# Cached attention for one new token: the softmax of a step in two halves, and the last V in two loads

## The chip, the cores and the metric

The kernel runs on one core of one Trainium2 chip. A core has a matrix engine (TensorE, PE in the profile, with its weight loads listed as PEld), a vector engine (VectorE, DVE), a scalar engine (ScalarE, ACT), GpSimd (POOL) and SyncE (SP), which here only issues transfers. Sixteen transfer engines move data between device memory and the core. SBUF is the core's working memory, PSUM the memory in which matmuls leave their results. [...]

The metric is the device time of a whole execution in microseconds (us). The profile is of one execution.

## The reference

```python
xn = _layernorm(x)                         # x: 2 x 1 x 512
q  = (xn @ wq)                             # 2 batches x 32 heads x 128
scores = einsum("bhqd,bhkd->bhqk", q, k_cache) * (Dh ** -0.5)   # 8192 rows a head
p  = softmax(scores, axis=-1)
o  = einsum("bhqk,bhkd->bhqd", p, v_cache)
out = x + o.reshape(B, Sq, H * Dh) @ wo + relu(xn @ w1) @ w2
```

There is one query per batch and head, against 8192 rows of K and V of 128 numbers each, in bfloat16. K and V are 134 MB each, and each number is used once. The weights `wq`, `wo`, `w1` and `w2` are 12 MB together.

## The kernel before

The 64 pairs of batch and head are taken four at a time (`U = 4`), so there are 16 steps (`NP`). In a step the 128 partitions hold the four heads, 32 partitions each, and every partition holds 256 of its head's rows (`KB = 256`, index `kk`). One load of 8.4 MB brings a step's K into the buffer `ks`, another its V into `vs`. There is one buffer for each, not two.

**SP's queue** (lines 161 to 188) issues all the loads, in this order: K of step t, V of step t, K of step t+1 and so on. Before K of step t it waits for the last transposes of step t-1 (semaphore `pT[7]`, line 167). Before V of step t it waits for the last V matmul of step t-1 (`sW`, line 177). The last K is loaded in two halves. After the last transposes the weights `w1`, `w2` and `wo` go into the room of `ks` (lines 179 to 184).

**A step on PE** (lines 286 to 319). First 256 transposes of K (line 265), in 32 groups of eight, each group into one of four PSUM tiles `tp`. VectorE and ScalarE copy the groups to SBUF as `kT` (line 394, ScalarE the groups in `ON_ACT`). From group 28 on, scores of early groups are woven in (`LAG`). Then the remaining scores (line 272): 256 small matmuls that write into `Sc`, two banks of PSUM, 128 values of `kk` in each, four heads beside each other. For the softmax, VectorE takes each head's maximum over the first 128 `kk` after group 15 of the scores (`EARLY`, `sS0`) and over the other 128 after group 31 (`sS`), into the two columns of `mcol` (line 441). PE transposes both columns (line 303), VectorE reduces them to one negated maximum per head, `mx` (line 446), PE spreads it over the partitions (line 306), ScalarE copies it to `nm` (line 488) and makes four exps over 256 columns each (line 492), which also give the sum of each partition in `RS`. When all four are done (`sP`), PE runs the 256 V matmuls (line 311) into one accumulator `ot`. After the last one SP may issue the next V, and ScalarE copies the result to `OTf` (line 502).

GpSimd copies each step's four queries to `q4` (line 227) after the scores of the step before are done. It then also raises `dKb`, the second K semaphore, for those steps whose K comes in one load (line 229).

**The end** (lines 321 to 387). PE adds up the denominators over partitions (line 324), VectorE takes the reciprocal and multiplies (lines 453 and 456), while PE works on the first dense layer (line 338). Then come a transpose, a selection, and the projections by `w2` and `wo` (line 365), which are added into the same PSUM columns, and the store.

The order is written out by hand: there is no planner, and each engine's program is one loop over steps with semaphore waits. The loops of PE, VectorE and ScalarE keep the values to wait for in registers (`counters`, `advance`).

Of the kernel before, what the change touches and what calls it, by code (L numbers as in the profile page):

```python
# [11 lines left out]
U = 4  # L12
EG = 8
NG = 32
REP = 16
LAG = 28
EARLY = 16
ON_ACT = (0, 3, 5)


# [1 line left out]
def kernel(  # L22
# [79 lines left out]

    prm = sb([P, KB, U], bf16, "prm")
    mcol = sb([P, 2], bf16, "mcol")
    mx = sb([1, U], bf16, "mx")
    nm = sb([P, U], f32, "nm")
    RS = sb([P, NP], f32, "RS")
    OTf = sb([P, N], f32, "OTf")
    RD = sb([P, N], f32, "RD")
    OTn = sb([P, Bsz, H], bf16, "OTn")  # L110
    Ob = sb([H, Bsz, Dh], bf16, "Ob")
    OX = sb([P, WJ, Bsz], bf16, "OX")
# [8 lines left out]

    S = Sc[:].rearrange("p (k u) -> p k u", u=U)
    trp = ms[0:1, 0:P].bitcast(bf16)
    bc = ms[:, 480:480 + U]


    dX, dO, dQ, dW1, dW2 = sem("dX"), sem("dO"), sem("dQ"), sem("dW1"), sem("dW2")
    dKa, dKb, dV = sem("dKa"), sem("dKb"), sem("dV")
    sG, sI, sQ, sQ1 = sem("sG"), sem("sI"), sem("sQ"), sem("sQ1")
    sV, sA, sE = sem("sV"), sem("sA"), sem("sE")  # L130
    sS0, sS, sT, sB, sW = sem("sS0"), sem("sS"), sem("sT"), sem("sB"), sem("sW")
    pT = [sem(f"pT{e}") for e in range(HG)]
    kR = [sem(f"kR{e}") for e in range(HG)]
    sM, sX, sP, sO, sN = sem("sM"), sem("sX"), sem("sP"), sem("sO"), sem("sN")
# [26 lines left out]

    @(lambda f: f(nc.sync))
    def _(sp):
        for t in range(NP):
            rows = slice(t * P, (t + 1) * P)
            if t > 0:
                sp.wait_ge(pT[HG - 1], NH * t)
            if t < NP - 1:
                sp.dma_start(ks[:], K_all[rows, :]).then_inc(dKa, 16)
            else:  # L170
                for i, d in enumerate((dKa, dKb)):
                    half = slice(i * SLOT // 2, (i + 1) * SLOT // 2)
                    sp.dma_start(ks[:, half], K_all[rows, half]).then_inc(d, 16)
            if t == 0:
                sp.wait_ge(sQ, 2)
            else:
                sp.wait_ge(sW, t)
            sp.dma_start(vs[:], V_all[rows, :]).then_inc(dV, 16)
        sp.wait_ge(pT[HG - 1], NH * NP)
        sp.dma_start(w1_sb, B_w1.rearrange("(p kt) f -> p kt f", kt=KT)).then_inc(dW1, 16)  # L180
        sp.dma_start(w2_sb, B_w2.rearrange("(p j) n -> p j n", j=FJ)).then_inc(dW2, 16)
        for c in range(NC):
            sl = slice(cuts[c], cuts[c + 1])
            sp.dma_start(wo_sb[:, sl, :], wo_v[:, sl, :]).then_inc(piece[c][0], 16)
        sp.wait_ge(sE, 1)
        sp.dma_start(
            out.rearrange("b s (c p) -> (b s c) p", p=P), osb[:]
        ).then_inc(dO, 16)


    def counters(eng, kind):
        regs = [nc.alloc_register(kind, f"count{i}_{kind.name}") for i in range(1 + NH)]
        eng.reg_mov(regs[0], 0)
        for i in range(NH):
            eng.reg_mov(regs[1 + i], i + 1)
        return regs[0], regs[1:]

    def advance(eng, h):
        for r in h:
            eng.reg_add(r, r, NH)  # L200

    @(lambda f: f(nc.gpsimd))
    def _(g):
# [19 lines left out]
        g.wait_ge(sV, 100)  # L223
        for t in range(NP):
            if t > 0:
                g.wait_ge(sS, t)
            g.tensor_copy(q4[:], qb[:, U * t:U * t + U]).then_inc(sQ1, 1)  # L227
            if t < NP - 1:
                g.wait_ge(dKa, 16 * (t + 1)).then_inc(dKb, 16)
        g.wait_ge(dO, 16).then_inc(sG, 1)  # L230


# [1 line left out]
    def _(pe):  # L234
# [33 lines left out]
        def scores(e):  # L268
            for i in range(EG):
                kk = e * EG + i  # L270
                n = min(REP, BK - kk % BK)
                t = pe.matmul(  # L272
                    Sc[:, U * kk:U * (kk + n)],
                    lhsT=kT[e][:, i, :],
                    rhs=rep(q4[:], n),
                    start=True,
                    stop=True,
                )
            if e == EARLY - 1:
                t.then_inc(sS0, 1)  # L280
            if e == NG - 1:
                t.then_inc(sS, 1)

        reg, h = counters(pe, mybir.EngineType.PE)
        with pe.Fori(16, NL + 1, 16) as n16:
            pe.reg_add(reg, reg, 1)
            pe.wait_ge(dKa, n16)
            pe.wait_ge(sQ1, reg)
            for e in range(NG):
                if e == NG // 2:  # L290
                    pe.wait_ge(dKb, n16)
                if e >= 4:
                    pe.wait_ge(kR[(e - 4) % HG], h[(e - 4) // HG])
                transposes(e)
                if e >= LAG:
                    scores(e - LAG)
            for e in range(NG - LAG, NG):
                if e >= NG - 4:
                    pe.wait_ge(kR[e % HG], h[e // HG])
                scores(e)  # L300
            pe.wait_ge(sM, reg)
            for i in range(2):
                t = pe.transpose(trp[:, i * P:(i + 1) * P], mcol[:, i:i + 1], identb[:])  # L303
            t.then_inc(sT, 1)
            pe.wait_ge(sX, reg)
            pe.matmul(bc, lhsT=onesb[:], rhs=mx[:], start=True, stop=True).then_inc(sB, 1)  # L306
            pe.wait_ge(sP, reg)
            pe.wait_ge(sO, reg)
            pe.wait_ge(dV, n16)
            for kk in range(KB):  # L310
                t = pe.matmul(  # L311
                    ot[:, 0:U * REP],
                    lhsT=vs[:, kk * Dh:(kk + 1) * Dh],
                    rhs=rep(prm[:, kk, :], REP),
                    start=(kk == 0),
                    stop=(kk == KB - 1),
                )
            t.then_inc(sW, 1)
            advance(pe, h)

        pe.wait_ge(sI, 2 + U)
        dbp = Sc[:, 0:N].rearrange("p (t u) -> p t u", u=U)
        for u in range(U):
            t = pe.matmul(dbp[:, :, u], lhsT=onesh[:, u, :], rhs=RS[:], start=True, stop=True)  # L324
        t.then_inc(sH, 1)
        for k in range(KT):
            pe.matmul(
# [16 lines left out]
                )  # L344
        i.then_inc(sF, 1)

        pe.wait_ge(sV, 102)
        tO = tp[0][0:H, 0:Bsz, :]
        for b in range(Bsz):
            t = pe.transpose(tO[:, b, :], OTn[:, b, :], identb[:])  # L350
        t.then_inc(sH, 1)
        pe.wait_ge(sV, 103)
        for dq in range(DQ):
            t = pe.matmul(
                ox.rearrange("p (b j) -> p b j", b=Bsz),
# [19 lines left out]
        pe.wait_ge(dW2, 16)  # L375
        for j in range(FJ):
            project(w2_sb, j, hT)
        pe.wait_ge(sV, 104)
        for c in range(NC):
            pe.wait_ge(*piece[c])  # L380
            for j in range(cuts[c], cuts[c + 1]):
                t = project(wo_sb, j, OX, j == WJ - 1)
        t.then_inc(sH, 1)
        pe.wait_ge(sV, 105)
        pe.transpose(
            tp[1][0:Bsz * KT, 0, :], yT[:].rearrange("p b c -> p (b c)"), identb[:]
        ).then_inc(sH, 1)
# [10 lines left out]
    def _(v):  # L398
# [31 lines left out]
            tpq.rearrange("p l (g b) -> p l g b", b=Bsz),  # L430
        ).then_inc(sV, 93)

        reg, h = counters(v, mybir.EngineType.DVE)
        with v.Fori(0, NP):
            v.reg_add(reg, reg, 1)
            kcopies(v, False, h)
            for i, (lo, hi, s) in enumerate(((0, EARLY * EG, sS0), (EARLY * EG, KB, sS))):
                v.wait_ge(s, reg)
                for u in range(U):
                    own = slice(u * HP, (u + 1) * HP)  # L440
                    m = v.tensor_reduce(  # L441
                        out=mcol[own, i:i + 1], in_=S[own, lo:hi, u], axis=AX.X, op=ALU.max
                    )
            m.then_inc(sM, 1)
            v.wait_ge(sT, reg)
            v.tensor_reduce(  # L446
                out=mx[:], in_=trp.rearrange("o (i u m) -> o u i m", i=2, u=U),
                axis=AX.XY, op=ALU.max, negate=True,
            ).then_inc(sX, 1)
            advance(v, h)  # L450

        v.wait_ge(sH, 1)
        v.reciprocal(out=RD[:], in_=Sc[:, 0:N]).then_inc(sV, 1)
        v.wait_ge(sV, 101)
        v.wait_ge(sO, NP + 1)
        v.tensor_tensor(
            out=OTn[:].rearrange("p b h -> p (b h)"), in0=OTf[:], in1=RD[:], op=ALU.mult
        ).then_inc(sV, 1)
        v.wait_ge(sF, 1)
        v.tensor_scalar(  # L460
# [15 lines left out]
    def _(a):  # L476
# [2 lines left out]
            out=rstd[:], in_=mv[:, 1:2], func=ACTF.Sqrt, bias=eps_t[:Bsz], scale=1.0  # L479
        ).then_inc(sA, 1)  # L480

        a.copy(nm[:, 0:1], eps_t[:]).then_inc(sO, 1)
        reg, h = counters(a, mybir.EngineType.Activation)
        with a.Fori(0, NP) as t:
            a.reg_add(reg, reg, 1)
            kcopies(a, True, h)
            a.wait_ge(sB, reg)
            a.copy(nm[:], bc).then_inc(sN, 1)  # L488
            a.wait_ge(sN, reg)
            for u in range(U):  # L490
                own = slice(u * HP, (u + 1) * HP)
                x = a.activation(  # L492
                    out=prm[own, :, u],
                    in_=S[own, :, u],
                    func=ACTF.Exp,
                    bias=nm[own, u:u + 1],
                    scale=1.0,
                    accum_out=RS[own, bass.ds(t, 1)],
                )
            x.then_inc(sP, 1)  # L500
            a.wait_ge(sW, reg)
            a.copy(OTf[:, bass.ds(t * U, U)], ot[:, 0:U]).then_inc(sO, 1)  # L502
            advance(a, h)
# [1 line left out]
_INS = ['A_x', 'A_k_cache', 'A_v_cache', 'A_wq', 'A_wo', 'B_x', 'B_w1', 'B_w2']  # L505
_OUTS = [((2, 1, 512), 'bfloat16')]
# [25 lines left out]
```

## Time and profile before

| | |
|---|---|
| median of 8 runs | 696.02 us (692.76 to 698.48) |
| profiled execution | 698.76 us |
| its span, first to last instruction | 696.7 us |
| mean granted clock of PE | 0.893 |
| busy: PE, DVE, ACT | 548.3, 259.7, 269.9 us |
| read from device memory | 280.50 MB, 403 GB/s over the span |
| K transposes (line 265) | 4096, 247.4 us busy |
| scores (line 272) | 4096, 136.4 us busy |
| V matmuls (line 311) | 4096, 155.2 us busy; PE idle before them 59.3 us |
| exps (line 492) | 64, 817 ns each, of which 248 ns is the reading of the accumulator |
| maxima over 128 columns (line 441) | 128, 290 ns each |
| from issue to landing, K and V | median 24.8 and 22.2 us |

Busy time is the sum over instructions of one engine. [...] A line of a group ends with the idle time of the engine just before that group and with what ended it. In the row of slices, the span is cut in 40 equal parts and each digit is a share in tenths. `SPq` is SP's queue of transfers, and a wait there is a load that could not be issued yet. The chain is followed back from the last instruction, at each step to what released it.

### The profile page before, as it was taken

The numbers are of one execution on the slowest core, as the hardware profiler recorded it, in microseconds if no ns is written. First come the engines' busy times: TensorE is split into PE (matmuls) and PEld (weight loads), VectorE is DVE, ScalarE is ACT, GpSimd is POOL, SyncE is SP. The second block draws the span as 40 slices with busy tenths as digits, with TensorE's granted clock in tenths as the row PEclk, the third lists the DMA queues.
The fourth block names the chain that finished last, engine by engine and source line by source line (L and its number), as shares of the span: only waits on it lengthen the run. The fifth ranks groups of instructions, "written<-read, shape, count | busy, mean of one in ns | idle before, by whom it ended". The sixth has DMA issues, their size and how long they took to land.

```text
span 696.7 us, 26564 instructions
## 1 busy us (share of the span) xinstructions
PE 548.3 (79%) x12635; PEld 533.4 (77%) x12635; DVE 259.7 (37%) x481; ACT 269.9 (39%) x371; POOL 7.1 (1%) x30
## 2 busy tenths in 40 slices
PE   2494986967699696868879686977969696796968
PEld 0294986967688696868879686977969696796967
DVE  1071360715326071623517062441707153160711
ACT  1061433616333361624335262433527153251710
POOL 2000000000000000000000000000000000000000
PEclk9786998989989898989989898998989898898987
DMA  9999599999989999999999999899999999999992
GB/s 399 444 416 412 201 421 421 421 440 440 380 365 421 421 421 421 421 425 418 421 410 433 421 421 421 361 421 421 444 399 421 421 421 421 403 391 410 421 397 117
DMA packets 5789, 280.64 MB, mean 403 GB/s; under 512 B 658, under 2 KB 660, under 8 KB 916
## 3 DMA queue, kind: packets, MB, share of 16 engines
q1 hardware_dynamic: 5776, 280.50, 94.8%
q8 instruction: 8, 0.13, 0.1%
q10 hardware_dynamic: 4, 0.00, 0.0%
q14 instruction: 1, 0.01, 0.0%
HBM read 280.50 MB, written 0.00 MB: 403 GB/s over the span
## 4 chain that ended last, share of the span: by engine, by line
DMA 47%; PE 47%; ACT 3%; issue 1%; DVE 1%; ACTq 0%; SPq 0%
DMA ks<-in_A_k_cache_dram 47%; PE tp L265 34%; PE Sc L272 6%; PE ot L311 6%; ACT prm L492 2%; PE Sc L365 1%; DVE mcol L441 1%; ACT L394 1%; PE ms L338 0%; ACT kT L394 0%; DVE mx L446 0%; PE ms L303 0%; PE Sc L324 0%; PE ms L306 0%; ACT nm L488 0%
## 5 line engine op out<-in xcount | busy, mean ns | idle before, releaser
L394 DVE COPY kT<-tp 128x1024 bf16<-128x1024 bf16 x320 | 211.0, 688 | 295.0 <-PE tp L265 289.4
L265 PE MATMUL tp<-identb,ks 128*128 128x128 bf16 x4096 | 247.4, 222 | 38.7 <-DMA ks<-in_A_k_cache_dram 35.8
L265 PEld LDWEIGHTS tp<-identb,ks 128*128 128x128 bf16 x4096 | 237.2, 100 | 40.8 <-DMA ks<-in_A_k_cache_dram 37.3
L394 ACT COPY kT<-tp 128x1024 bf16<-128x1024 bf16 x192 | 190.1, 1013 | 86.7 <-PE tp L265 84.6
L311 PE MATMUL ot<-prm,vs 128*128 128x64 bf16 x4096 | 155.2, 207 | 59.3 <-ACT prm L492 59.3
L311 PEld LDWEIGHTS ot<-prm,vs 128*128 128x128 bf16 x4096 | 153.3, 108 | 60.6 <-ACT prm L492 60.6
L272 PE MATMUL Sc<-q,kT 128*128 128x64 bf16 (+8 forms) x4096 | 136.4, 191 | 4.6 <-issue 4.6
L272 PEld LDWEIGHTS Sc<-q,kT 128*128 128x128 bf16 x4096 | 132.4, 98 | 4.7 <-issue 4.7
L441 DVE TENSOR_REDUCE mcol<-Sc 32x1 bf16<-32x128 f32 x128 | 37.1, 290 | 89.8 <-PE Sc L272 88.5
L488 ACT COPY nm<-ms 128x4 f32<-128x4 f32 x16 | 2.6, 163 | 160.8 <-PE ms L306 160.8
L502 ACT COPY OTf<-ot 128x4 f32 x16 | 2.6, 162 | 158.0 <-PE ot L311 158.0
L492 ACT ACTIVATE prm<-Sc,nm 32x256 bf16<-32x256 f32 x64 | 52.3, 818 | 2.7
L394 ACT ACT_TABLE_LOAD x16 | 20.5, 1283 | 2.8 <-issue 2.7
L303 PE MATMUL ms<-identb,mcol 128*1 128x128 bf16 x32 | 4.5, 222 | 20.7 <-DVE mcol L441 20.7
L303 PEld LDWEIGHTS ms<-identb,mcol 128*1 128x1 bf16 x32 | 1.4, 81 | 22.1 <-DVE mcol L441 22.1
L492 ACT ACTIVATION_READ_ACCUMULATOR prm<-Sc,nm x64 | 15.8, 248 | 0.0
L244 PE MATMUL ot<-vs,xz 128*16 128x512 bf16 x32 | 9.4, 466 | 8.1 <-DMA vs<-in_A_wq_dram 8.1
L244 PEld LDWEIGHTS ot<-vs,xz 128*16 128x16 bf16 x32 | 3.3, 105 | 13.8 <-issue 11.4
L306 PEld LDWEIGHTS ms<-mx,onesb 1*128 1x128 bf16 x16 | 1.5, 92 | 11.2 <-DVE mx L446 11.2
L227 POOL COPY q<-qb 128x4 bf16<-128x4 bf16 x16 | 3.0, 188 | 620.4 <-PE Sc L272 601.2
L306 PE MATMUL ms<-mx,onesb 1*128 1x4 bf16 x16 | 2.8, 174 | 8.1 <-DVE mx L446 8.1
L446 DVE TENSOR_REDUCE mx<-ms 1x4 bf16<-1x256 bf16 x16 | 6.6, 412 | 5.9 <-PE ms L303 5.9
(51 smaller groups left out, 33.4 us busy)
## 6 DMA issues: line engine op xcount, KB each, us to landing
ks<-in_A_k_cache_dram SPq DMA_DIRECT2D x2, 4096.0 KB, 18.6
vs<-in_A_wq_dram SPq DMA_DIRECT2D x1, 4096.0 KB, 12.2
ks<-in_B_w_dram SPq DMA_DIRECT2D x2, 1792.0 KB, 11.8
ks<-in_A_wo_dram SPq DMA_DIRECT2D x1, 2304.0 KB
ks<-in_A_wo_dram SPq DMA_DIRECT2D x1, 1024.0 KB, 21.0
ks<-in_A_wo_dram SPq DMA_DIRECT2D x1, 512.0 KB, 21.8
vs<-in_A_v_cache_dram SPq DMA_DIRECT2D x16, 22.2
ks<-in_A_wo_dram SPq DMA_DIRECT2D x1, 256.0 KB, 21.9
```

Source lines behind the costliest of these rows:

```text
L227: g.tensor_copy(q4[:], qb[:, U * t:U * t + U]).then_inc(sQ1, 1)
L244: i = pe.matmul(qp, lhsT=xz[:, kt, Z - g * Bsz:Z - g * Bsz + QG * Bsz], rhs=vs[:, (kt * QG + g) * 512:(kt * QG + g + 1) * 512], start=(g = ...
L265: t = pe.transpose(tp[e % 4][:, i, :], ks[:, kk * Dh:(kk + 1) * Dh], identb[:])
L272: t = pe.matmul(Sc[:, U * kk:U * (kk + n)], lhsT=kT[e][:, i, :], rhs=rep(q4[:], n), start=True, stop=True,)
L303: t = pe.transpose(trp[:, i * P:(i + 1) * P], mcol[:, i:i + 1], identb[:])
L306: pe.matmul(bc, lhsT=onesb[:], rhs=mx[:], start=True, stop=True).then_inc(sB, 1)
L311: t = pe.matmul(ot[:, 0:U * REP], lhsT=vs[:, kk * Dh:(kk + 1) * Dh], rhs=rep(prm[:, kk, :], REP), start=(kk == 0), stop=(kk == KB - 1),)
L365: t = pe.matmul(fin[:, k * Bsz:(k + 1) * Bsz], lhsT=w[:, j, k * P:(k + 1) * P], rhs=x[:, j, :], start=False, stop=(last and k == KT - 1),)
L394: fn(kT[e][:], tp[e % 4][:]).then_inc(kR[e % HG], 1)
L441: m = v.tensor_reduce(out=mcol[own, i:i + 1], in_=S[own, lo:hi, u], axis=AX.X, op=ALU.max)
L446: v.tensor_reduce(out=mx[:], in_=trp.rearrange("o (i u m) -> o u i m", i=2, u=U), axis=AX.XY, op=ALU.max, negate=True,).then_inc(sX, 1)
L492: x = a.activation(out=prm[own, :, u], in_=S[own, :, u], func=ACTF.Exp, bias=nm[own, u:u + 1], scale=1.0, accum_out=RS[own, bass.ds(t, 1)],)
```

## The change

The two banks of `Sc` become two halves of the softmax, each with its own maximum, its own four exps over 128 columns, its own sums (`RS` gets a second index) and its own accumulator in `ot` (`oh[:, i, :]`). The first half's small transpose stands after group 21 of the scores and its spread after group 25 (`TR`). PE starts the V matmuls when the first half's exps are done. Ahead of the first of them it does the second half's transpose, and before V matmul 32 (`BC`) its spread. In the middle of the 256 matmuls it waits for the second half's exps. At the end of a step ScalarE keeps the maxima of both halves in `NM`.

After the last step the halves are joined: with the smaller negated maximum `lo`, the factors are F = exp(lo - NM), and numerators and denominators of both halves are multiplied by F and added. This takes six VectorE operations between the denominators and `OTn` for the two before, two more ahead of them, and one exp over 128 columns.

The last V comes in two loads of half the columns, as the last K already does. V has two semaphores for that, and GpSimd raises the second for all other steps, after a wait for V.

```diff
-EARLY = 16
+TR = (21, 25)
+BC = 32
...
+        def load(tile, src, t, d):
+            rows = slice(t * P, (t + 1) * P)
+            cols = [slice(0, SLOT)] if t < NP - 1 else [
+                slice(i * SLOT // 2, (i + 1) * SLOT // 2) for i in range(2)
+            ]
+            for c, i in zip(cols, d):
+                sp.dma_start(tile[:, c], src[rows, c]).then_inc(i, 16)
...
-                g.wait_ge(sS, t)
+                g.wait_ge(sS, 2 * t)
             g.tensor_copy(q4[:], qb[:, U * t:U * t + U]).then_inc(sQ1, 1)
             if t < NP - 1:
-                g.wait_ge(dKa, 16 * (t + 1)).then_inc(dKb, 16)
+                for d in (dK, dV):
+                    g.wait_ge(d[0], 16 * (t + 1)).then_inc(d[1], 16)
...
+        def turn(i):
+            pe.wait_ge(sM, g[i])
+            pe.transpose(
+                trp[:, i * P:(i + 1) * P], mcol[:, i:i + 1], identb[:]
+            ).then_inc(sT, 1)
+
+        def spread(i):
+            pe.wait_ge(sX, g[i])
+            pe.matmul(
+                bc[:, i, :], lhsT=onesb[:], rhs=mx[:, i, :], start=True, stop=True
+            ).then_inc(sB, 1)
...
                 scores(e)
-            pe.wait_ge(sM, reg)
-            for i in range(2):
-                t = pe.transpose(trp[:, i * P:(i + 1) * P], mcol[:, i:i + 1], identb[:])
-            t.then_inc(sT, 1)
-            pe.wait_ge(sX, reg)
-            pe.matmul(bc, lhsT=onesb[:], rhs=mx[:], start=True, stop=True).then_inc(sB, 1)
-            pe.wait_ge(sP, reg)
+                if e == TR[0]:
+                    turn(0)
+                if e == TR[1]:
+                    spread(0)
             pe.wait_ge(sO, reg)
-            pe.wait_ge(dV, n16)
             for kk in range(KB):
+                i, first = divmod(kk, KB // 2)
+                if first == 0:
+                    pe.wait_ge(sP, g[i])
+                    if i == 0:
+                        turn(1)
+                    pe.wait_ge(dV[i], n16)
+                if kk == BC:
+                    spread(1)
                 t = pe.matmul(
-                    ot[:, 0:U * REP],
+                    oh[:, i, :],
...
+            for i in range(2):
+                a.wait_ge(sB, g[i])
+                a.copy(nm[:, i, :], bc[:, i, :]).then_inc(sN, 1)
+                a.wait_ge(sN, g[i])
+                for u in range(U):
+                    own = slice(u * HP, (u + 1) * HP)
+                    k = slice(i * KB // 2, (i + 1) * KB // 2)
+                    x = a.activation(
+                        out=prm[own, k, u],
+                        in_=S[own, k, u],
+                        func=ACTF.Exp,
+                        bias=nm[own, i, u:u + 1],
+                        scale=1.0,
+                        accum_out=RS[own, i, bass.ds(t, 1)],
+                    )
+                x.then_inc(sP, 1)
+            a.copy(NM[:, :, bass.ds(t * U, U)], nm[:]).then_inc(sC, 1)
...
+        v.tensor_tensor(out=lo[:], in0=NM[:, 0, :], in1=NM[:, 1, :], op=ALU.min).then_inc(sV, 1)
...
+        v.tensor_tensor(out=df[:], in0=both(lo[:]), in1=NM[:], op=ALU.subtract).then_inc(sV, 1)
...
+        v.tensor_tensor(out=den[:], in0=DF[:, 0, :], in1=DF[:, 1, :], op=ALU.add).then_inc(sV, 1)
...
+        v.reciprocal(out=RD[:], in_=den[:]).then_inc(sV, 1)
...
+        v.tensor_tensor(out=G[:], in0=both(RD[:]), in1=F[:], op=ALU.mult).then_inc(sV, 1)
...
+        v.tensor_tensor(out=OG[:], in0=OTf[:], in1=G[:], op=ALU.mult).then_inc(sV, 1)
...
+        a.activation(out=F[:], in_=df[:], func=ACTF.Exp, scale=1.0).then_inc(sA, 1)
```

## The prediction

> **What bounds the kernel now.** I read the profile page first, then the waits of SP's queue, the chain in order of time, the timeline of one step, and the landings of the loads. The page's slices:
>
> ```profile
> PEclk9786998989989898989989898998989898898987
> DMA  9999599999989999999999999899999999999992
> ```
>
> The transfers fill the run: 280.5 MB. They stop in three ways: once early (fifth slice), at the end (last slice), and in crumbs. PE's clock falls in every step. What SP, which issues all loads on one queue, waits for:
>
> ```profile
> SPq L178 <- PE ot L311: 341.3, 15, 28.1
> SPq L169 <- PE tp L265: 249.5, 14, 27.6
> ```
>
> V waits for the end of the step's V matmuls (PV, L311), K for the end of its transposes (L265). Each has one buffer. The chain that ended last, in order of time (start, length):
>
> ```profile
> 135.41 25.61 DMA ks<-in_A_k_cache_dram
> 161.07 14.75 PE tp L265 x232
> ...
> 177.93 24.43 DMA ks<-in_A_k_cache_dram
> 202.41 13.13 PE tp L265 x232
> ...
> 217.65 24.68 DMA ks<-in_A_k_cache_dram
> ```
>
> So a step is: K lands, transposes, next K issued, and so on. Twelve such periods, from the transposes' start at 120.17 to that at 604.46, average 40.36 us. The chain can't say whether K itself was late or stood behind V in the queue, so I took each load's landing from the trace's semaphore writes of the transfer engines (sixteen to a load). A load issued 2 us or more before its predecessor landed follows it by 19.33 us: two loads, 38.7 us, is the floor of a step. Between the landing at 119.5 and that of the last K at 644.1 there are 26 loads and 22 us beyond 26 x 19.33: 17 us before V loads, which were issued only 0 to 2 us ahead or after the K landed, 5 us before K loads. The timeline of one step shows why V is late:
>
> ```profile
> 135.22 7.19 PE L272 MATMUL Sc<-q,kT 128*128 128x64 bf16 x232
> 135.41 0.33 SPq L169 DMA_DIRECT2D ks<-in_A_k_cache_dram  x1
> 142.44 1.20 DVE L441 TENSOR_REDUCE mcol<-Sc 32x1 bf16<-32x128 f32 x4 [2.70 <-PE Sc L272]
> ...
> 148.36 9.11 PE L311 MATMUL ot<-prm,vs 128*128 128x64 bf16 x256 [3.70 <-ACT prm L492]
> 157.50 0.33 SPq L178 DMA_DIRECT2D vs<-in_A_v_cache_dram  x1
> ...
> 161.07 2.14 PE L265 MATMUL tp<-identb,ks 128*128 128x128 bf16 x21 [3.60 <-DMA ks<-in_A_k_cache_dram]
> ```
>
> Scores end at 142.4; PE stands 5.9 us through maximum and exp; PV takes 9.1 us, the first 2.8 at half clock; then V goes out. PE then waits 3.6 us for K.
>
> [...] 19.33 us apart when queued, about 21.1 from issue into an empty queue. [...] the granted clock was 0.50 from 161.4 to 164.8. [...] The halves are exactly the two banks of Sc, and the reduces during the second half's scores take 0.29 us like those after it.
>
> **The change part by part.** T is the end of the scores without the change.
>
> 1. *Into the score stream* go one transpose (0.22 us) and one spread (0.17): T becomes T' = T + 0.4. Their inputs: scores(15) is 16 groups x 0.245 = 3.9 us before T, the four reduces take 1.2, the transpose stands 10 groups (2.45 us) before T, so it doesn't wait; the [1,128] reduce has no row (256 elements take 0.41; 0.2 to 0.41, I take 0.3), and the spread stands four groups (1 us) later. First exps start at T' - 0.9.
> 2. *Exp over 128 columns.* No row. The 256-column one is 0.82 us, of which 0.25 is reading the accumulator. [...] Bounds: 0.54 (all but the read halves) to 0.82 (nothing shrinks). Four: 2.85 (2.1 to 3.3). First half ready at T' + 1.95.
> 3. *PE then* waits for the second maximum (T' + 1.25, earlier), transposes (0.25) and starts PV at T' + 2.25. At full clock 0.0303 us each (232 scores in 7.04): kk=32 at T' + 3.2, spread 0.17, copy and gap 0.35, four exps 2.85: second half ready at T' + 6.6. First PV half ends T' + 6.3, so 0.3 stall; PV ends T' + 10.5. Now it is T + 15.1 (157.5 - 142.4). Gain 4.2 us. If the 2.2 us idle still drops the clock, up to 1.6 of it is lost.
> 4. *NM copies, POOL's wait on V and relay of its semaphore, more counters.* POOL's next q copy is queued behind the V wait; V lands some 4 us before the scores end, so nothing; if V came later than T, q and hence the transposes would wait. NM copy 0.17 us on ACT, hidden by PV; uncovered, 16 x 0.17 = 2.7.
> 5. *The end.* Denominator matmuls with 32 columns for 16: +0.2. DVE has six operations from the denominator to OTn for two, 0.78 now, about 2.0 (0.2 to 0.3 each, reciprocal 0.56). They lie beside the 3.5 us of W1 matmuls: nothing; uncovered, 1.2. F's exp may bring a table load of 1.28, still under that cover.
> 6. *Last V in halves:* one more issue, 0.4; on the path nothing, because V then lands before PV wants it.
>
> *Where the gain goes.* In the middle V now goes out at 16.9 + 7.05 + 0.4 + 10.5 = 34.9 us after the transposes' start, some 4.5 ahead of K's landing: its 17 us of gaps vanish. But then V lands 19.33 after K, and what is late next is K. PE waits about 5 us for K instead of 0 to 3.6, so its transposes start at half clock in each step. Three steps of the present trace are like that (161.07, 402.69, 604.46; waits of 2.9 to 3.6): start to K issue 16.86 us for 15.24. The lead over V's landing is then 19.33 - 0.35 - 16.86 less the spread between transfer engines (0.3 to 2.2 us): 0 to 1.8, where V is today. Eleven loads issued with such a lead took 22.6 us on average to their last landing (21.5 to 24.1). So a period is 16.86 + 22.6 + 0.35 = 39.8 us: **0.55 of the 40.36, not 1.66, comes back**.
>
> *Head.* Step 0 ends PV at 79.06 with transfers idle from 71.9 to 80.3 (the fifth slice): V1 goes out 4.2 earlier, less about 1 because the half clock there lasts into PV: 3.3. The transposes at 120.17 come at 116.9.
>
> *Tail.* From the start at 604.46 it is now 39.9 to the end of PV 14, 16.2 to the last transposes, 7.05 + 15.2 to the end of PV 15 (682.86), 13.9 to the end: 92.3. After: 34.9 + 16.2 + 7.05 + 0.4 + 10.5 + 13.9 + 0.2 = 83.1. The transfers allow it: last K 16.9 + 23.3 = 40.2, V 59.5, the weights 19.1 later (now 665.3 to 684.5) 78.6, and 3.6 to the end, 82.2. Gain 9.2.
>
> *Sum:* 116.9 + 12 x 39.8 + 83.1 = 677.6 for the span of 696.7, 19.1 less: 3.3 head, 6.6 middle, 9.2 tail. The profiled execution took 698.76 (2.06 around the span), so 679.7 for its like. It stood 2.7 above the median of 696.02; taking 19.1 from that gives **677 us**.
>
> **Rivals.**
>
> *A, the middle streams.* If PE is warm at K's landing, or transfer engines stay together, K's lead is 2 us or more and a period is 38.7: 116.9 + 464.4 + 83.1 = 664.4, median 664. For it: ten of the thirteen transposes were warm. Against: a wait of 5 us is longer than any that stayed warm.
>
> *B, the halves don't overlap.* If the small chain costs PE what it saves (exps at 0.82, cold PV, a stall in the scores): PV ends only 2 us earlier. Head 1, middle still about 4 (a lead of 2 suffices for V), tail 4: 9 less, 687. For it: the accumulator read, 0.25, is paid eight times. Against: the first half's chain has 3.9 us of scores over it. The change not doing what it says is this case carried on: no gain, 696.
>
> *C, K's turn gets worse (slower).* One mechanism: the longer wait lengthens the half clock (a 6 us stretch, as before the first transposes, costs 2.8 in place of 1.6) and the engines' spread persists, so that K takes 24.1 to land. The step from 161.07 to 202.41, cold with V in time, did take 41.34. A period of 18.0 + 24.1 + 0.35 = 42.5 gives 709, median 708. It decides from 41.4 a period, where 116.9 + 12 x 41.4 + 83.1 = 696.8. Against: the other two cold steps took about 39.9 and 40.5.
>
> **How the numbers follow.** Forecast 0.64 (periods of 39.2 to 40.6: its own range is 670 to 687), A 0.18, B 0.11 including no gain at all (0.03), C 0.07 (0.02 of it within 0.5% of before). 0.5% is about what a measurement of this kernel can tell from no change. Faster: 0.64 + 0.18 + 0.08 = 0.90; within: 0.05; slower: 0.05. Range: A's 664 as the lower end; the upper from a period of 40.8, or B: 689.
>
> **What the profile after would show.** Right: PE's wait for the first exps about 2 us, V issued about 35 after a step's first transpose, transfers idle some 5 us in the fifth slice, half clock at the start of nearly all transposes, K issues about 17 us after them and periods of 39 to 40.5. Wrong: most transposes warm (A), SP's V issues still at K's landing (B), K flights of 24 (C). The least sure term is the period: 0.1 us of it is 1.2 us of the result.

## The result and the profile after

The changed kernel takes 684.9 us (median of 10 runs, 677.54 to 687.46) against 694.7 us for the kernel before in the same comparison: a ratio of 0.985, 95% interval 0.9825 to 0.9875. It is faster, by about half of what was forecast. The profiled execution took 679.66 us, 5.2 below that median, with a span of 677.9.

The page's slices of the kernel after, in the same form as before:

```profile
PEclk9796997897989989897998979899897989989997
DMA  8999699999999999999999999999999999999996
```

The transfers still pause in the fifth slice. The crumbs in the middle don't show at this width, but they are still there, as the loads will show.

What SP's queue waited for, in the kernel after (one line now issues both K and V):

```profile
SPq L181 <- PE tp L278: 336.0, 15, 27.6
SPq L181 <- PE ot L338: 261.8, 15, 25.8
```

Before, the larger of the two was V's wait for PV (341.3 us against 249.5). Now it is K's wait for the transposes.

One step of the kernel after, from its timeline (start, length, engine, line, operation; in brackets the idle time before it and what ended that):

```profile
175.62 4.81 PE L285 MATMUL Sc<-q,kT 128*128 128x64 bf16 x152
175.82 0.33 SPq L181 DMA_DIRECT2D ks<-in_A_k_cache_dram  x1
...
182.10 0.54 ACT L545 ACTIVATE prm<-Sc,nm 32x128 bf16<-32x128 f32 x1
...
183.31 1.20 DVE L471 TENSOR_REDUCE mcol<-Sc 32x1 bf16<-32x128 f32 x4 [2.42 <-PE Sc L285]
...
184.66 0.22 PE L297 MATMUL ms<-identb,mcol 128*1 128x128 bf16 x1 [1.38 <-DVE mcol L471]
...
184.81 1.14 PE L338 MATMUL ot<-prm,vs 128*128 128x64 bf16 x32
...
185.98 6.93 PE L338 MATMUL ot<-prm,vs 128*128 128x64 bf16 x224
...
192.95 0.33 SPq L181 DMA_DIRECT2D vs<-in_A_v_cache_dram  x1
```

The first exps begin at 182.10, while PE is still at the scores. PE stands only 1.4 us between scores and PV, PV runs through both halves without a stall and at full clock (granted 1.00 from 184.85 to 192.95), and V goes out 9.7 us after the last score (183.27). Before it was 15.1.

The chain in order of time, kernel after, the same lines as before:

```profile
158.41 15.30 PE tp L278 x232
...
175.82 21.85 DMA ks<-in_A_k_cache_dram
197.71 14.46 PE tp L278 x232
...
214.28 22.09 DMA ks<-in_A_k_cache_dram
236.42 15.53 PE tp L278 x232
```

The transposes that took 13.13 us in most steps, at a granted clock of 1.00, now take 14.5 to 16.0 in every step that waits for K: they start at half clock, 0.50 to 0.53 over their first 3 us. K lands sooner after its issue (21.85 and 22.09 us here, 24.43 and 24.68 before). Counted as landings are below, K of steps 3 to 14 takes 21.6 us on average here and 23.7 before, and the V ahead of it has 1.0 us left when K is issued, for 4.1 before. Twelve periods average 39.93 us (40.36 before).

The landings of the loads, from the semaphore writes of the transfer engines, give the account below. A load has sixteen such writes, and here and in what follows its landing is the middle one; PE is released by the last, 0.1 to 3.1 us later (in the step above the last came at 197.67, the transposes start at 197.71). A gap is what a load took beyond 19.33 us after the one ahead of it, summed over the 13 K loads and the 12 V loads from K of step 2 to K of step 14 (steps count from 0). The other columns are the first transpose of the third step (head), twelve periods from there (middle), and the rest of the span (tail).

| profile | head | middle | tail | span | gaps before V | gaps before K |
|---|---|---|---|---|---|---|
| before, first (the one shown) | 120.17 | 484.3 | 92.2 | 696.7 | 15.9 | 3.1 |
| before, second | 114.49 | 486.2 | 91.4 | 692.1 | 15.9 | 5.0 |
| before, third | 119.84 | 483.7 | 91.3 | 694.9 | 14.9 | 2.7 |
| before, fourth | 114.49 | 486.1 | 92.0 | 692.6 | 18.1 | 3.5 |
| after, first | 117.18 | 479.1 | 81.6 | 677.9 | 0.5 | 14.9 |
| after, second | 117.33 | 477.7 | 85.2 | 680.2 | 0.6 | 13.3 |
| after, third | 118.73 | 479.4 | 83.8 | 681.9 | 1.6 | 13.0 |

V's gaps went, from 16.2 to 0.9 us on average, and some two thirds of that came back before K, from 3.6 to 13.7.

### The profile page after: what moved, and what is told of

It reads as the page before. It is cut to its first block, busy times and chain, and to the rows that moved or that the text cites. A ratio compares the mean times of both kernels' runs of the same rounds, so it can differ in the third digit from the quotient of the medians.

```text
span 677.9 us, 26929 instructions
## 1 busy us (share of the span) xinstructions
PE 549.9 (81%) x12651; PEld 534.5 (79%) x12651; DVE 264.5 (39%) x503; ACT 293.3 (43%) x532; POOL 7.2 (1%) x30
## 4 chain that ended last, share of the span: by engine, by line
PE 49%; DMA 48%; issue 1%; ACT 1%; DVE 1%; SPq 0%; ACTq 0%
DMA ks<-in_A_k_cache_dram 48%; PE tp L278 38%; PE Sc L285 5%; PE ot L338 4%; PE Sc L395 1%; DVE mcol L471 1%; PE ms L368 1%; ACT L424 0%; ACT kT L424 0%; PE ms L297 0%; PE Sc L351 0%; PE ms L303 0%; SPq L169 0%; PE ms L384 0%; PE tp L380 0%
## 5 line engine op out<-in xcount | busy, mean ns | idle before, releaser
L278 PE MATMUL tp<-identb,ks 128*128 128x128 bf16 x4096 | 268.1, 232 | 84.2 <-DMA ks<-in_A_k_cache_dram 82.3
L278 PEld LDWEIGHTS tp<-identb,ks 128*128 128x128 bf16 x4096 | 258.1, 105 | 86.3 <-DMA ks<-in_A_k_cache_dram 84.0
L285 PE MATMUL Sc<-q,kT 128*128 128x64 bf16 (+8 forms) x4096 | 142.0, 192 | 0.6 <-issue 0.6
L338 PE MATMUL ot<-prm,vs 128*128 128x64 bf16 x4096 | 133.2, 194 | 0.1
L338 PEld LDWEIGHTS ot<-prm,vs 128*128 128x128 bf16 x4096 | 129.2, 98 | 2.0 <-issue 0.2
L545 ACT ACTIVATE prm<-Sc,nm 32x128 bf16<-32x128 f32 x128 | 68.9, 538 | 5.4
L540 ACT COPY nm<-ms 128x4 f32<-128x4 f32 x32 | 5.2, 163 | 137.5 <-PE ms L303 137.5
L545 ACT ACTIVATION_READ_ACCUMULATOR prm<-Sc,nm x128 | 32.0, 250 | 0.0
L478 DVE TENSOR_REDUCE mx<-ms 1x4 bf16<-1x128 bf16 x32 | 8.9, 279 | 17.7 <-PE ms L297 17.7
L257 PEld LDWEIGHTS ot<-vs,xz 128*16 128x16 bf16 x32 | 3.1, 99 | 13.4 <-issue 10.5
L303 PE MATMUL ms<-mx,onesb 1*128 1x4 bf16 x32 | 5.6, 174 | 0.0
```

Source lines behind the costliest of these rows:

```text
L257: i = pe.matmul(qp, lhsT=xz[:, kt, Z - g * Bsz:Z - g * Bsz + QG * Bsz], rhs=vs[:, (kt * QG + g) * 512:(kt * QG + g + 1) * 512], start=(g = ...
L278: t = pe.transpose(tp[e % 4][:, i, :], ks[:, kk * Dh:(kk + 1) * Dh], identb[:])
L285: t = pe.matmul(Sc[:, U * kk:U * (kk + n)], lhsT=kT[e][:, i, :], rhs=rep(q4[:], n), start=True, stop=True,)
L303: pe.matmul(bc[:, i, :], lhsT=onesb[:], rhs=mx[:, i, :], start=True, stop=True).then_inc(sB, 1)
L338: t = pe.matmul(oh[:, i, :], lhsT=vs[:, kk * Dh:(kk + 1) * Dh], rhs=rep(prm[:, kk, :], REP), start=(first == 0), stop=(first == KB // 2 - 1),)
L478: v.tensor_reduce(out=mx[:, i, :], in_=trp[:, i * P:(i + 1) * P].rearrange("o (u m) -> o u m", u=U), axis=AX.X, op=ALU.max, negate=True,). ...
```

## The experiments

Theory K is the forecast's: once V is in time, K's way round (transposes at half clock, issue, landing) sets the step. Theory V: V is still too late. Theory R: the transfer engines can't do a step faster. The time of the kernel before is that of the same comparison throughout.

**The changed kernel again**, no edit.

> The changed kernel once more, beside the others. Theory K (a step is now the way round from K's landing over the transposes at half clock, 17.2 us, to the next K's landing, 22.2 to 23): about 685 us, ratio to before 0.985, and in the profile a period of 39.9 to 40.4 with K issued less than 2 us before V lands and V issued 4 us or more before K lands. Theory V (V is still issued too late): V's lead under 2 us. Theory R (the transfer engines can't do a step faster than this): loads follow each other by about 20 us whatever their lead.

682.19 us, ratio 0.9835 (0.9787 to 0.9883). From the third step on V was issued 3.0 us or more before K landed (4.4 mostly), and from the fourth on K between 0.5 us after and 2.5 us before V landed; periods average 39.81, just under the 39.9 to 40.4 expected. This is theory K's picture, and theory V's is not seen.

**A warm clock, first try.** 150 small matmuls at the head of a step, on the changed kernel:

```diff
+            for _ in range(150):
+                pe.matmul(
+                    ms[:, 320:384], lhsT=identb[:], rhs=identb[:, 0:64], start=True, stop=True
+                )
             pe.wait_ge(dK[0], n16)
```

> The changed kernel with 150 small matmuls into an unused corner of PSUM at the head of each step, before PE waits for K (about 4.5 us at full clock, in time that PE stood idle), so that PE's clock stays up. Their results are used nowhere. Theory K: transposes start at full clock, K goes out 15.3 to 15.6 us after the first transpose instead of 17.2, its lead over V's landing becomes about 3 us, a period becomes 38.7 to 39.3, and with 12 periods and 1.6 to 2.5 us lost in the last step the time is 668 to 676, ratio to before 0.963 to 0.973. Theories V and R: no gain in the middle, the fillers only cost their part in the last step: 685 to 689.

884.9 us, ratio 1.27: outside every expectation. Two lines of its profile, from the queues of the page and the waits:

```profile
q8 instruction: 144, 2.36, 1.2%
PE ms L311 <- issue: 128.8, 31, 6.0
```

The kernel before and the one after have 8 instruction packets in the whole run. Here there are 144, nine a step, with a loop of PE that is 300 instructions longer (weight loads included), and PE stands 129 us before the fillers alone without a wait that the profile shows (`issue`). That PE stood for these packets, as the next expectation has it too, is a reading of these two figures; the loop's length alone was not varied further. The run says nothing on the clock.

**A warm clock, second try**: the same time filled by 20 matmuls of 512 columns.

```diff
-            pe.wait_ge(dK[0], n16)
             pe.wait_ge(sQ1, reg)
+            for _ in range(20):
+                pe.matmul(ms[:], lhsT=identb[:], rhs=prm[:, 0:KB // 2, :], start=True, stop=True)
+            pe.wait_ge(dK[0], n16)
```

> The changed kernel with 20 wide matmuls (512 columns, about 0.22 us each, 4.3 us in all) into PSUM that nobody needs then, at the head of each step before PE waits for K; their results are used nowhere. The 150 small fillers of the run before made PE's program too long to stay loaded (144 instruction packets for 8, 132 us of issue waits before them), so they said nothing on the clock; 20 are 1.5% of a step's instructions. Theory K: transposes start at full clock, K goes out about 15.3 us after the first of them and not 17.2, its lead over V's landing grows to 1.7 to 3.4 us, a period becomes 38.7 to 39.2 in place of 39.9, the last step loses 1.6 to 3: 670 to 677, ratio to before 0.965 to 0.975. Theories V and R: no gain in the middle, 684 to 689.

670.12 us, ratio 0.9627 (0.9588 to 0.9666), as theory K said. PE's wait for K, from the waits of the kernel after, and of this one:

```profile
PE tp L278 <- DMA ks<-in_A_k_cache_dram: 82.3, 14, 9.7
```

```profile
PE tp L278 <- DMA ks<-in_A_k_cache_dram: 22.0, 13, 2.8
```

In eight of thirteen steps K now goes out 15.2 us after the first transpose or sooner, in five still 16.9, with 2.0 to 2.8 us of waiting left behind the fillers and 14.75 us for the 232 transposes that take 13.13 in most of the others. The gaps before K fall from 13 to 15 us to 4.8, those before V stay at 0.8, and twelve periods take 469.9 us, 39.16 each. The head also came earlier (114.17), the tail is 84.2. Useless work in PE's idle time makes the kernel 2% faster than the changed one (670.12 us for 682.19), with a mean granted clock of 0.971, for 0.915 in the changed kernel's first profile. So the half clock at K's landing, which the changed kernel has in all thirteen steps, is what took most of the gain back, and it did so through K's issue. About half of the 4.8 us that are left before K stands behind steps that still start cold. The largest single gap, 1.5 us before K of step 14, does not, and its cause was not looked for.

**K earlier instead.** Every K in two halves on the changed kernel, the first issued when half of the transposes of the step before are done:

```diff
-            if t > 0:
-                sp.wait_ge(pT[HG - 1], NH * t)
-            load(ks, K_all, t, dK)
+            for i in range(2):
+                half = slice(i * SLOT // 2, (i + 1) * SLOT // 2)
+                if t > 0:
+                    sp.wait_ge(pT[HG - 1], NH * (t - 1) + NH // 2 * (i + 1))
+                sp.dma_start(ks[:, half], K_all[rows, half]).then_inc(dK[i], 16)
```

GpSimd then no longer raises `dK[1]`.

> The changed kernel with every K loaded in two halves, the first issued when the first 16 groups of the step before are transposed, so that K's issue comes some 7 us earlier and its landing is waited for by halves. The clock may still fall. Theory K: the queue never runs dry, a period is 38.7, the hole in the first step closes too (V1 would go out before K1 has landed), and the time is 654 to 664, ratio 0.942 to 0.956. Theory R: 680 to 686. Theory V: as now, 680 to 686, since V goes out at the same point of a step.

659.43 us, ratio 0.9504 (0.9466 to 0.9541). The page's line of the queue that carries the loads, after and here:

```profile
q1 hardware_dynamic: 5920, 280.50, 96.9%
```

```profile
q1 hardware_dynamic: 8080, 280.50, 99.1%
```

With 99.1% of the span there is nothing left to fill, and from the last half of K in step 2 to that in step 15 thirteen steps take 38.8 us each. Now V is in the queue in time, and PE waits for its data: one line of this run's waits, and one of its timeline.

```profile
PE ot L340 <- DMA vs<-in_A_v_cache_dram: 30.8, 14, 2.2
```

```profile
131.06 1.89 PE L340 MATMUL ot<-prm,vs 128*128 128x64 bf16 x32 [2.20 <-DMA vs<-in_A_v_cache_dram]
```

Theory R falls: the engines do a step in 38.8 us, as the 19.33 us of a load had said. No version of the study is faster. As PE's wait moved from K to V, so did the half clock: in steps 2 to 14 every transpose ran at full clock (in each, the 104 behind K's second half took 5.98 us), and the V matmuls at a granted mean of 0.71 to 0.83.

**The same edit on the kernel before**, with its softmax in one piece:

> The kernel before with every K loaded in halves in the same way, the softmax as before. Theory K: PV then ends some 7 us earlier against the landing of the next K's second half, V is in time even with the whole softmax ahead of PV, and a period is 38.7 here too: 656 to 668, ratio 0.945 to 0.962, at most 5 us behind the same edit of the changed kernel. Theory V (V's lateness by the softmax is what costs): V's 17 us remain, 685 to 692.

673.91 us, ratio 0.9711 (0.9672 to 0.9749), 14.5 us behind the same edit of the changed kernel where at most 5 had been expected, so the expectation missed. The timeline of PE in step 2, up to the start of step 3, shows why:

```profile
123.14 7.19 PE L267 MATMUL Sc<-q,kT 128*128 128x64 bf16 x232
131.62 0.27 PE L298 MATMUL ms<-identb,mcol 128*1 128x128 bf16 x2 [1.29 <-DVE mcol L436]
132.40 0.17 PE L301 MATMUL ms<-mx,onesb 1*128 1x4 bf16 x1 [0.51 <-DVE mx L441]
136.28 10.30 PE L306 MATMUL ot<-prm,vs 128*128 128x64 bf16 x256 [3.70 <-ACT prm L487]
146.48 1.95 PE L260 MATMUL tp<-identb,ks 128*128 128x128 bf16 x32
```

PE goes from PV straight to the next transposes, without a wait for K. Its own serial way (transposes, scores, 5.9 us standing at the softmax, PV partly at half clock: 10.30 us here, 8.1 at full clock in the kernel after) takes 38.4 to 39.8 us from one first transpose to the next, a mean of 39.14 by the landings of K. With K in time, PE's own way with the softmax stall in it is the bound of the kernel before. Of the 12.6 us between the two profiles' spans, the thirteen steps from K of step 2 to that of step 15 give 4.6 and the way from the last K to the end 7.6 (50.8 to 43.2). The larger part is thus the end, for which the expectation of at most 5 us left too little room. The two edits together are worth 34 us in this comparison; the softmax's 12 and K's 20 alone make 32, which these intervals can't tell from it.

**V late on purpose.** The 20 wide fillers on the changed kernel, placed between the last V matmul and V's signal:

```diff
+            for _ in range(20):
+                t = pe.matmul(ms[:], lhsT=identb[:], rhs=prm[:, 0:KB // 2, :], start=True, stop=True)
             t.then_inc(sW, 1)
```

> The same 20 wide fillers, but ahead of the signal that lets V go out, so that V is issued 4.3 us later than in the changed kernel, about as late as before the change; PE's clock is kept up as in the run with the fillers at the head of a step. Theory K with V's lead as the second limit: V is late again (0 to 1 us of lead, 1.2 to 1.7 us of gap), K is in time, a period is 39.9 to 40.4, and the ends of the last two steps come 4.3 us later each: 688 to 697, ratio 0.990 to 1.005. If V's time of issue does not matter while K's turn is the limit: 675 to 684, as the run with the fillers at the head plus the last steps' 4 to 6 us.

696.52 us, ratio 1.0033 (1.0011 to 1.0054), within theory K's first range. V's gaps are back at 13.3 us, K's fell to 3.2, twelve periods average 40.13, and the tail is 89.2. PE does the same work here as in the run with the wide fillers at the head; what differs in a step is that V goes out 4.3 us later (14.0 after the last score for 9.7). The two medians are 26 us apart. Of the 24.3 between the two profiles' spans, the head has 7.6, the middle 11.7 and the tail 5.0, in which one filling of 4.3 us more stands. V's and K's gaps take each other's place, and only a kernel that has neither is fast.

**The last V in one load**, the rest as in the changed kernel:

```diff
-            load(vs, V_all, t, dV)
+            sp.dma_start(vs[:], V_all[t * P:(t + 1) * P, :]).then_inc(dV[0], 16)
```

> The changed kernel with the last V in one load, and without GpSimd's wait for V; the softmax in halves as it is. All theories: the last V lands 1 to 3 us before or at PV's start, so the loads in halves are worth 0 to 2 us: 682 to 688, ratio 0.980 to 0.990.

GpSimd then no longer raises the second V semaphore, and PE waits for the first alone. 683.55 us, ratio 0.9847 (0.9804 to 0.9889): no difference from the changed kernel that these intervals can tell. In its profile the last write of the last V came at 654.4 us, 1.1 before PE began with it. The second part of the change is worth nothing measurable here.

**Both aids together**, K in halves and the wide fillers at the head:

> Both edits together: the changed kernel with K in halves and with the 20 wide fillers at the head of each step. Theory K says that the clock costs time only by making K's issue late: with K in halves the queue never runs dry, so a warm PE has nothing to give, and the fillers delay only the last step: 659 to 664, ratio to before 0.950 to 0.957 (K in halves alone: 0.950). If the half clock costs time in its own right: 648 to 655.

660.39 us, ratio 0.9525 (0.948 to 0.9569), against 0.9504 for K in halves alone. K in halves alone had left no transpose at half clock, so only the V matmuls could still gain: without the fillers they ran partly at half clock in all of the steps 2 to 14, with them in eight of the thirteen (mean granted clock of the profiled executions 0.932 and 0.959), and a step takes 38.8 us either way. So with K early the half clock costs nothing that these runs can tell, because the loads set the step.

**More profiles**, of the kernel before (three) and after (one), no edits:

> The kernel before against itself, for a second profile: ratio 1.000 within 0.005. If the period of 40.36 us and the tail of 92.3 us in the first profile are typical, they come again within 0.15 and 1 us; the first profiled execution stood 4 us above the median, so by theory K the period should now be about 40.0 to 40.2, with V's gaps the largest part of what is over 38.7.

> The kernel before, a third profile. The first had its third step's first transpose at 120.17 us, the second at 114.49, with 4.6 and 1.3 us in which PE had no instructions in the first step (issue). If the first profile was an unlucky one, the third lies near 114 to 116; if both kinds are common, anywhere from 114 to 121.

> The kernel before, a fourth profile, for the same question: 114 to 121, and 12 periods of 40.2 to 40.8 us.

> The changed kernel, a third profile: first transpose of the third step at 117.2 to 117.4 as in its first two, with an issue wait of about 3.8 us at the first small transpose in the scores; 12 periods of 39.8 to 40.3 us.

Before against before gave 1.0007 (0.9986 to 1.0028). The three single profiles took 696.91, 694.65 and, for the changed kernel, 683.7 us. The spans are in the table above. Two expectations missed: the second profile of before had periods of 40.52 us where theory K's 40.0 to 40.2 was expected, and the third of after a head of 118.73 (117.2 to 117.4 expected). The kernel before has two kinds of head, near 114.5 and near 120. PE's first step in the first and in the second profile of before, and in the first of after:

```profile
59.88 4.04 PE L272 MATMUL Sc<-q,kT 128*128 128x64 bf16 x79 [4.61 <-issue]
```

```profile
70.64 2.65 PE L311 MATMUL ot<-prm,vs 128*128 128x64 bf16 x82 [1.28 <-issue]
```

```profile
58.90 0.26 PE L297 MATMUL ms<-identb,mcol 128*1 128x128 bf16 x1 [3.79 <-issue]
```

In the first step six of the eight instruction packets come, between 39 and 77 us. Two profiles of before stood 4.6 us in the scores without a wait that the profile shows, two did not and stood about 1 us later on. In the kind without, the second packet came at 46.4 and 46.6 us, in the kind with it at 48.8 and 48.9. That PE stood for the packets is a reading of these times, not shown by a run. All three profiles of after wait 3.5 to 3.8 us, at the small transpose that now stands in the scores. Whether that transpose's place in the program makes the wait so constant was not tried.

## Why the prediction was right or wrong

- **What is late next: right.** The forecast said that V's gaps would vanish and K would be late in its turn, with PE cold at each landing, a period of 39.8 us and 0.55 us of 1.66 coming back. The periods are 39.93, 39.81 and 39.95, against 40.31 to 40.52 in the four profiles of before: 0.53 came back. The fillers at the head and the late V show both sides of it, and towards rival A's 38.7 is where it goes if the cause is taken away (39.16 with PE warm in eight of thirteen steps).
- **The cold start: right, somewhat short.** From the first transpose to K's issue it is 16.6 to 18.1 us, on average 17.3, for the 16.86 taken over. K's flight to the next start made up for it, 22.6 for 22.95. The forecast read its landings some 0.4 us early: a load into an empty queue took 21.5 us to its middle write (V of step 1 in two profiles of before), not 21.1. No sum rests on that.
- **The softmax in halves: right, its gain under-sized.** V goes out 9.7 us after the scores that now include both insertions (10.5 forecast), so with their 0.4 the gain is 5.0, not 4.2. The exps follow each other every 0.56 us. That is near the lower bound of 0.54. The 2.85 taken for four was the author's estimate between the bounds, which no trace of before showed: measured, 128 columns less are 0.28 us less, 2.2 ns a column. The exps also start 1.2 us before the scores end, not 0.9. Therefore it is the second maximum that PE waits for and not the first exps, 1.4 us and not 2.2, and the V matmuls run at full clock in all but one of the steps 2 to 14 (granted 1.00, in step 6 0.80; in all but three in the two other profiles). In the middle this should change nothing, since V had lead to spare; that was not tried apart.
- **The end and the extra operations: right.** From the end of PV 15 (663.7) to the last instruction it is 14.2 us, 14.1 forecast. The six operations lie under the W1 matmuls, and the last of them ends 1.3 us before PE asks for OTn.
- **The span: 677.6 forecast, 677.9 measured**, with a head of 117.2 (116.9), a middle of 479.1 (477.6) and a tail of 81.6 (83.1). That it fits to 0.3 is luck in part: middle and tail are off by 1.5 each, in opposite ways, and the next two profiles took 680.2 and 681.9. In the second, PE waited for the last weights, 2.5 us in three waits, and the tail was 85.2.
- **The median: too low, 677 for 684.9.** The step that failed is "taking 19.1 from that": the difference between a sum and one profiled execution was taken as the difference between medians. The head of that profile was one of two kinds: four profiles of before average 117.2, and three of after 117.7, so the 3.3 us of the head are not there; V of step 1 goes out at 75.8 to 77.5 us after the change, against 78.6 and 79.1 where the kernel before had the wait of 4.6 us, and 73.2 and 73.3 where it had not. The tail was 92.2 where the four average 91.7; after it averages 83.5, so 8.2 and not 9.2. The middle is 6.3 for 6.6. In all the profiles differ by 14.1 us (694.1 to 680.0), not 19.1, and the head alone makes 3.8 of those 5.0.
- **Still open:** the medians of the timed runs differ by 10 to 12 us, 2 to 4 less than the profiles do. The changed kernel's timed runs reach 687, and no profile caught one of these: the profiled executions took 679.66 to 683.7. Where that part of the forecast went is not shown.

## What to carry to other kernels

When two loads take turns in one queue and each has a single buffer, write down how long before its predecessor's landing each is issued: here freeing one of them earlier, V, passed the gap on to the other, V's from 16.2 to 0.9 us and K's from 3.6 to 13.7, until K was issued earlier too and a step took 38.8 us. A lead of 2.5 us was enough: in the seven profiles of the two kernels, loads issued that long before the middle landing of the one ahead followed it by 19.39 us on average, those with 1 to 2 us of lead by 20.4, and those with 0 to 1 us by 21.0. Look also at what a faster engine does with the time: here PE's waits for K at the transposes grew from 35.8 to 82.3 us in the whole run, the transposes after a wait started at a granted 0.50 to 0.53 and took 14.5 to 16.0 us for 13.13, and it is these that let the next K go. Before a forecast from a profile is taken off a median, look at several profiles of the kernel before: here the head of one stood 3 us above the mean of four and 6 us above the lowest.

## What the runs showed of the hardware that was not expected

- 150 more matmuls, with as many weight loads, in PE's loop turned 8 instruction packets into 144 and cost 203 us against the changed kernel (884.9 to 682.2). 20 wide ones, 4.49 us of a step, cost no packet (8 again).
- With the fillers at the head of a step, five waits of 2.0 to 2.8 us at K's landing led to a start at half clock (14.75 us for 232 transposes), and eight of 0 to 2.5 us did not (13.13 us or less): the length alone doesn't tell.
- Halving the columns of an exp from 256 to 128 took it from 0.817 to 0.538 us, both with the accumulator's 0.25: 2.2 ns per column, with inputs and outputs four elements apart. Whether the stride, the PSUM input or the sum makes it so was not tried.
